# A fused attention, MLP and gated MLP on one core: where loads, adding transfers and a store stand on their queues

## The chip, the core and the metric

The kernel runs on one core of a Trainium2 chip. Its time is the device time of one execution in microseconds (us). TensorE (PE in the profile) multiplies matrices, VectorE (DVE), ScalarE (ACT) and GpSimd (POOL) work on elements, and SyncE (SP) only issues transfers here. GpSimd issues transfers too. Each engine works through its own instructions in order, and so does the queue of issues on SyncE and on GpSimd: an issue that waits holds up those behind it on the same engine.

## The reference

Three stages follow each other, all in 32-bit floats. q, k and v are [4 batches, 8 heads, 576 positions, 64]; x then is [4, 576, 512].

```
s1 = 1/8 * mean4(q) @ mean4(k).T            # means over 4 neighbouring positions, 144 x 144
up = repeat(softmax(s1) @ mean4(v), 4)
s2 = where(|i - j| < 4, 1/8 * q @ k.T, -1e9)
x  = up + softmax(s2) @ v                    # heads side by side: [4, 576, 512]

xn = (x - mean(x)) / sqrt(var(x) + 1e-6) * g
x2 = x + relu(xn @ w_ch1) @ w_ch2            # 512 -> 2048 -> 512

xk = mu_k * x2 + (1 - mu_k) * previous(x2)   # previous position
xr = mu_r * x2 + (1 - mu_r) * previous(x2)
out = sigmoid(xr @ w_r) * (relu(xk @ w_k)**2 @ w_v)   # 512 -> 1024 -> 512
```

## The kernel before

The 2304 positions (4 x 576) are cut into six chunks of 384, `c` = 0 to 5. Activations lie with features on the partitions. Each product of the two MLPs is made of three matmuls with operands split into a high and a low part (`mm3`, L203 to L206).

**Attention** is done in units `(c, hp)`, one for each chunk and each pair of heads (`hp` = 0 to 3), 24 in all. A unit (`unit`, L283) is a generator that gives the engines back at each `yield`. It makes the scores of the mean branch (tile `scd`, L333, from `kd`, the k summed over four positions) and of the local window (`sc`, L337), softmax on VectorE and ScalarE (`P`, `Pd`), transposes (`T`, `PT`, `tp`, `PdT`), and at last the product with v (`av`: L403 with `v`, L412 with `vd`, the v summed over four). Two units are under way at a time. The first chunk's four units run before the MLP starts; those of chunk c + 1 are mixed into the MLP of chunk c by class `Attn` and `slot`.

**Loads of a unit** are issued by SyncE: `load_qk` (L222: tiles `q` and `kz`), `load_v` (L231, tile `v`). `q` and `v` have two buffers each. In `unit` both are called at the start of a unit for the next one, so the load of v for unit u + 1 waits until `av` of unit u - 1 has read its buffer.

**kd and vd** are made for each batch and pair of heads by four transfers each (`sums`, L241): r = 0 is a plain load on SyncE, r = 1 to 3 are adding transfers on GpSimd's queue, each of which waits for the one before it to land. Seven buffers hold them (L237, L238); 16 pairs are made, four of them in the first chunk by sums on VectorE and GpSimd (`first_k`, `first_v`). A unit starts the sums for the unit two places ahead and takes a step of it four times (`step`). New batches begin in chunks 0, 1, 3 and 4.

**Weights** of the first MLP arrive raw (512 KB loads, `raw`, L124 for pairs and L129 for the last ones) and are converted by `conv_gen` in four steps on ScalarE and VectorE: L80, L81, L84, L85, and split into high and low (L88, L91). That goes on during the first chunk's attention and the first chunk of the MLP. Raw pairs and converted weights share 16 buffers (`wpool`). Two pairs are loaded ahead (`AHEAD`); `fetch` then asks for a pair at every second conversion.

**The MLP** of a chunk is `emit_l1` (hidden tile f: `h_ps`, then `hh` on ScalarE L589 and `hl` on VectorE L590) and `emit_l2` (into four accumulators `acc`), for f = 0 to 15. At a chunk's end `emit_x2` (L604) forms x2: VectorE scales `acc` into `x2t` (L609, two buffers), GpSimd adds it to x (L610), and one transfer on SyncE stores all four parts (L611, 768 KB) to `x2d`. The second MLP (from L792) reads `x2d` back, with its own weights that `pre_b` and `load_b` prepare.

A scheduler sets the order of the instructions on each engine from the order in which they are written. An instruction that is passed to `in_order(True, ...)` keeps its written place; others may move past their neighbours on their engine.

Of the kernel before, what the change touches and what calls it, by code (L numbers as in the profile page):

```python
# [23 lines left out]
N = 96 * NG  # L24
NCH = B * S // N
NHP = H // 2
# [3 lines left out]
KT = DM // 128  # L30
# [8 lines left out]
def tile_block(ctx: ExitStack, tc: tile.TileContext, qw, kw, kf, kr, vw, vr, vec, mask, w1, w2, wk, wv, wr, out):  # L39
    nc = tc.nc  # L40
# [15 lines left out]
    x2d = dram.tile([128, KT, B * S], F32, name="x2d")  # L56
# [10 lines left out]
    def in_order(on, ins):  # L67
        if on:
            tc.keep_in_program_order(ins)
# [5 lines left out]
    def decode(raw, pinned=False):  # L75

        top = raw.bitcast(U8).rearrange("p (n t) -> p n t", t=8)[:, :, 3]
        rm = stg.tile([128, 2, 512], U32, tag="stg", name="rm", bufs=RB)
        ru, m = rm[:, 0], rm[:, 1]
        in_order(pinned, nc.scalar.activation(ru.bitcast(F32), raw.rearrange("p (n t) -> p n t", t=2)[:, :, 1].bitcast(F32), AF.Copy, scale=2.0 ** -112))  # L80
        in_order(pinned, nc.vector.tensor_scalar(m, ru, 0x80000000, None, op0=ALU.bitwise_and))  # L81
        yield ru.bitcast(F32)
        low = m.bitcast(U8).rearrange("p (n t) -> p n t", t=4)[:, :, 0]
        in_order(pinned, nc.scalar.activation(low, top, AF.Copy, scale=1.0 / 32.0, bias=-31.0 / 64.0))  # L84
        in_order(pinned, nc.vector.scalar_tensor_tensor(ru, ru, 3, m, op0=ALU.logical_shift_left, op1=ALU.bitwise_or))  # L85

    def split_hi(hi, w):
        return nc.scalar.copy(hi, w)  # L88
# [4 lines left out]
    def wtiles(nm):  # L93
        return [wpool.tile([128, 4, 512], F32R, tag="w", name=f"{nm}{t}") for t in "hl"]
# [7 lines left out]
    def pieces_w12():  # L102
        for p in range(4):
            yield from (("w1", p, k) for k in range(KT))
            yield from (("w2", f // 4, f % 4) for f in range(max(4 * p - 1, 0), 4 * p + 3 if p < 3 else NF))

    def conv_gen():
        keys = list(pieces_w12())
        late_keys = [k for k in keys if k[:2] == ("w2", 3)]
        raws, todo = {}, iter([k for k in keys if k not in late_keys])  # L110

        def fetch():
            key = next(todo, None)
            while key in raws:
                key = next(todo, None)
            if key is None:
                return
            nm, p, k = key
            src = w1s[:, :, 1024 * p:1024 * p + 1024] if nm == "w1" else w2s[:, 4 * p:4 * p + 4, :]
            t = wpool.tile([128, 2, 1024], I32, tag="w", name="raw")  # L120
            for i in range(2):
                raws[nm, p, k + i] = t[:, i]
            for i in range(2):
                in_order(len(raws) < 18, nc.sync.dma_start(t[:, i], src[:, k + i]))  # L124

        def fetch_late(key):
            if key in late_keys:
                t = stg.tile([128, 1024], I32, tag="stg", name="raw", bufs=RB)
                nc.sync.dma_start(t, w2s[:, 12 + key[2], :])  # L129
                raws[key] = t  # L130

        for _ in range(ORDER.count("w")):
            fetch()
            yield
        for _ in range(AHEAD - ORDER.count("w")):
            fetch()
        last = None
        for n, key in enumerate(keys + [None]):
            pin = n < PINNED
            if last:  # L140
                in_order(pin, split_hi(h, w))
            if key:
                nm, p, k = key
                W = W1 if nm == "w1" else W2
                if p not in W:
                    W[p] = wtiles(f"{nm}_{p}")
                g = decode(raws[key], pin)
                w1st = next(g)
            yield
            if key:  # L150
                next(g, None)
            if last:
                in_order(pin, split_lo(h, l, w))
                done.add(last)
            if key:
                h, l, w = W[p][0][:, k, :], W[p][1][:, k, :], w1st
            last = key
            if n % 2 == 1 or n > 24:
                fetch()
            if n + 1 < len(keys):  # L160
                fetch_late(keys[n + 1])
            yield
# [45 lines left out]


    loaded, kds, vdt, vts = {}, {}, {}, {}  # L210
    qds, adding, firsts, raw_k, means = {}, {}, [], {}, {}
    xt, xsum, stage = {}, {}, {}
    av_user, multiplied = [], set()
    PT = pone.tile([128, 2 * NG, 4, 24], F32, name="PT")
# [4 lines left out]
    def runs(c):  # L219
        return [(2 * c + i) // 3 for i in range(2)]  # L220
# [10 lines left out]
    def load_v(c, hp):  # L231
        v = pin.tile([128, NG, 2, D], F32, tag="v", name="v")
        in_order(c == 0, nc.sync.dma_start(v, vw[hp, :, NG * c:NG * c + NG]))
        vts[c, hp] = v
# [6 lines left out]
    def sums(c, hp):  # L241

        new = [(b, *sum_tiles(b, hp)) for b in dict.fromkeys(runs(c)) if (b, hp) not in kds]
        for r in range(4):
            for b, kd, vd in new:
                eng, op = (nc.gpsimd, {"accum_op": ALU.add}) if r else (nc.sync, {})
                in_order(c <= 1 and r > 0, eng.dma_start(kd, kr[b, hp, r], **op))  # L247
                in_order(c <= 1 and r > 0, eng.dma_start(vd, vr[b, hp, r], **op))  # L248
            yield

    def first_k(hp):

# [7 lines left out]
    def first_v(hp):  # L260
        t = xp.tile([128, KT, N], F32, tag=("ah", "al")[hp % 2], name="vr", bufs=1).rearrange("p k n -> p (k n)")[0:KD, 0:1024].rearrange("p (r t d) -> p r t d", r=4, t=2)
        in_order(True, nc.sync.dma_start(t, vr[0, hp].rearrange("r p t d -> p r t d")))
        nc.gpsimd.tensor_tensor(t[:, 0:2], t[:, 0:2], t[:, 2:4], op=ALU.add)
        nc.gpsimd.tensor_tensor(vdt[0, hp], t[:, 0], t[:, 1], op=ALU.add)
# [13 lines left out]
    def mean_of(c, hp):  # L278
        if hp == 0:
            means[c] = ps_h.tile([128, 512], F32, tag="h", name="mean")  # L280
        nc.tensor.matmul(means[c][:, 0:N], ones_r.bitcast(F32), xt[c][:, hp, :], start=hp == 0, stop=hp == NHP - 1)

    def unit(c, hp, nxt):  # L283
        if (c, hp) not in qds:
            prep(c, hp)
        if nxt is not None:
            if nxt not in loaded:
                load_qk(*nxt)
                if nxt[0] == 0:
                    first_k(nxt[1])  # L290
            if nxt not in vts:
                load_v(*nxt)
                if nxt[0] == 0:
                    first_v(nxt[1])
        i = units.index((c, hp)) + 2
        far = units[i] if i < len(units) else None
        if far is not None and far not in adding:
            adding[far] = sums(*far)
        step = lambda: next(adding[far], None) if far is not None else None
        step()  # L300
        new = c == 0 or runs(c)[1] != runs(c - 1)[1]
        q, k = loaded.pop((c, hp))
        v = vts.pop((c, hp))
        if hp == 0:
            xt[c] = xp.tile([128, NHP, N], F32, tag="x", name="x")
        x = xt[c]
        i = hp % 2
        P = Ps[i]
        qd = qds.pop((c, hp))
        kd = [kds[b, hp] for b in runs(c)]  # L310
        vd = [vdt[b, hp] for b in runs(c)]
# [22 lines left out]
        for n in range(NG):  # L334
            for j in range(4):
                o = 24 * j
# [14 lines left out]
            prep(*nxt)  # L351
        yield 900
        stage[c, hp] = 1
        step()
        nc.vector.tensor_reduce(mx[:, 0:2 * NG], Pl, axis=AX.X, op=ALU.max)
        yield 320
        nc.vector.tensor_tensor(Pl, Pl, mx[:, 0:2 * NG].unsqueeze(2).to_broadcast([128, 2 * NG, WIN]), op=ALU.subtract)
# [6 lines left out]
        for j in range(2):  # L364
            nc.scalar.activation(Pd[:, j, :], Pd[:, j, :], AF.Copy, scale=m[:, j:j + 1])
        yield 400
        step()
        nc.vector.tensor_reduce(sm[:, 0:2 * NG], P[:, :, 0:WIN + 1], axis=AX.X, op=ALU.add)
        nc.vector.reciprocal(mx[:, 0:2 * NG], sm[:, 0:2 * NG])
        yield 500  # L370
# [1 line left out]
        yield 340  # L372
        while c + hp > 0 and units[units.index((c, hp)) - 1] not in multiplied:
            yield GAP
        step()
        T = pat.tile([128, 2 * NG, 32], F32, tag="T", name="T", bufs=1)
        nc.vector.transpose(T, P)  # L377
        yield 370
# [18 lines left out]
        yield GAP  # L397
        if c == 0 and hp > 0:
            mean_of(c, hp - 1)
        av = ps_at.tile([128, 512], F32, tag="av", name="av")  # L400
        for n in range(NG):
            for h in range(2):
# [36 lines left out]
    units = [(c, hp) for c in range(NCH) for hp in range(NHP)]  # L439
# [164 lines left out]
    def emit_x2(c):  # L604
        x = xt.pop(c)
        y = rstd.pop(c)
        for o in range(KT):
            t = xp.tile([128, N], F32, tag="x2", name="x2t")
            nc.vector.tensor_tensor(t, acc[o][:, 0:N], y, op=ALU.mult)  # L609
            nc.gpsimd.tensor_tensor(x[:, o, :], t, x[:, o, :], op=ALU.add)  # L610
        nc.sync.dma_start(x2d[:, :, N * c:N * c + N], x)  # L611

    class Feeder:
        def __init__(self, steps):
# [24 lines left out]
    for i in range(2):  # L639
        eng = nc.gpsimd if i else nc.vector  # L640
# [11 lines left out]
    for o in ORDER:  # L652
# [8 lines left out]
            nc.sync.dma_start(vec_t, vec)  # L661
        else:
            next(conv)
    adding.update((u, iter(())) for u in units[0:NHP])
    first = Attn(None, 0)
    i = 0
    while not first.over():
# [124 lines left out]
    for c in range(NCB):  # L792
        for f in range(NK):
            ps = bank()
            wh, wl = WK[f // 4]
            o = 128 * (f % 4)
            for k in range(KT):
                mm3(ps[:, 0:NB], wh[:, k, o:o + 128], wl[:, k, o:o + 128], xk[0][:, k, :], xk[1][:, k, :], k == 0, k == KT - 1)
            r = bp.tile([128, NB], F32, tag="kr", name="kr", bufs=3)
# [4 lines left out]
            kr = r  # L804
# [3 lines left out]
        nxt = Feeder(mix(c + 1, 0)) if c + 1 < NCB else Feeder(iter(()))  # L808
# [101 lines left out]
```

## Time and profile before

| what | value |
|---|---|
| median of 3 runs | 795.38 us (795.38 to 796.32) |
| the profiled execution | 795.89 us |
| its span, first to last instruction | 794.1 us |
| TensorE busy | 752.4 us |
| VectorE, ScalarE, GpSimd busy | 513.0, 370.7, 99.3 us |
| mean granted clock of TensorE | 0.987 of 2.4 GHz |
| moved by transfers | 78.79 MB |

Busy times of different engines overlap. A span of one engine's idle time tells what it waited for last; the chain of waits follows the work that ended last back to the start. The granted clock has two levels, 1.2 and 2.4 GHz; a mean of 0.9 over a stretch says that a fifth of it ran at the lower one.

### The profile page before, as it was taken

How to read it: one execution, taken by the hardware profiler on the slowest of the kernel's cores; microseconds unless marked ns; L12 is line 12 of the kernel's file. 1: busy time of each engine (PE TensorE's matmuls, PEld its weight loads, DVE VectorE, ACT ScalarE, POOL GpSimd, SP SyncE). 2: the span in 40 equal slices, each digit the busy share in tenths (PEclk: the TensorE clock that was granted, in tenths of full speed). 3: DMA queues.
4: the chain of work that ended last, by engine and by line, in shares of the span. 5: the costliest groups of instructions: out<-in, count | busy, mean ns of one | idle time of the engine just before them, and what ended most of it. 6: DMA issues, size and time to landing. Idle time of an engine off the chain costs nothing.

```text
span 794.1 us, 13626 instructions
## 1 busy us (share of the span) xinstructions
PE 752.4 (95%) x5380; PEld 722.6 (91%) x5380; DVE 513.0 (65%) x1015; ACT 370.7 (47%) x839; POOL 99.3 (13%) x124
## 2 busy tenths in 40 slices
PE   3669979899999999999999999999999999999998
PEld 2449869799999999999999999999999999999998
DVE  6777688766546655655555446625969596868664
ACT  4577587645434453445345324524444353525140
POOL 2334123413340001110100010001000000000000
PEclk9969999999999999999999999999999999999999
DMA  8894786446633421553134003403020202010101
GB/s 242 248 249 85 217 232 167 118 139 169 161 71 129 128 96 67 145 138 100 67 101 142 1 1 133 133 1 120 6 75 11 70 1 80 1 40 1 41 1 40
DMA packets 49023, 78.79 MB, mean 99 GB/s; under 512 B 5568, under 2 KB 34880, under 8 KB 48960
## 3 DMA queue, kind: packets, MB, share of 16 engines
q1 hardware_dynamic: 40320, 72.61, 29.0%
q0 software_dynamic: 8640, 5.32, 5.1%
q8 instruction: 42, 0.69, 0.3%
q14 instruction: 21, 0.17, 0.1%
HBM read 63.22 MB, written 14.68 MB: 98 GB/s over the span
## 4 chain that ended last, share of the span: by engine, by line
PE 83%; DMA 5%; ACT 5%; DVE 4%; issue 1%; SPq 1%; POOL 0%; ACTq 0%; POOLq 0%
PE b_ps L206 11%; PE b_ps L204 10%; PE b_ps L205 10%; PE h_ps L204 8%; PE h_ps L205 7%; PE h_ps L206 7%; PE acc L204 7%; PE acc L205 7%; PE acc L206 7%; PE av L403 2%; DMA raw<-in_w 2%; PE scd L333 1%; DMA vd<-in_vr 1%; DMA q<-in_qw 1%; PE sc L337 1%; ACT PT L381 1%
## 5 line engine op out<-in xcount | busy, mean ns | idle before, releaser
L590 DVE SCALAR_TENSOR_TENSOR hl<-h_ps,hh 128x384 fp32r<-128x384 f32 x96 | 53.0, 553 | 94.3 <-ACT hh L589 94.0
L589 ACT ACTIVATE hh<-h_ps 128x384 fp32r<-128x384 f32 x96 | 46.9, 489 | 104.3 <-PE h_ps L206 103.9
L206 PE MATMUL b_ps<-k,wbl 128*128 128x384 f32 x192 | 64.1, 334 | 0.0
L204 PE MATMUL b_ps<-xk,wbh 128*128 128x384 f32 x192 | 64.1, 334 | 0.0
L205 PE MATMUL b_ps<-xk,wbh 128*128 128x384 f32 x192 | 64.1, 334 | 0.0
L206 PE MATMUL b_ps<-xk,wbl 128*128 128x384 f32 x192 | 64.1, 334 | 0.0
L204 PE MATMUL b_ps<-k,wbh 128*128 128x384 f32 x192 | 64.1, 334 | 0.0
L205 PE MATMUL b_ps<-k,wbh 128*128 128x384 f32 x192 | 64.1, 334 | 0.0
L820 DVE RECIPROCAL e<-e 128x384 f32<-128x384 f32 x24 | 61.1, 2544 | 0.1
L610 POOL TENSOR_TENSOR x<-x2t,x 128x384 f32<-128x384 f32 x24 | 23.9, 1058 | 254.4 <-DVE x2t L609 132.2
L737 ACT ACTIVATE mixa<-x2in,vec_t 128x384 f32<-128x384 f32 x48 | 28.1, 612 | 39.7 <-DVE xr L740 33.9
L248 POOL DMA_DIRECT2D vd<-in_vr x36 | 35.1, 991 | 90.9 <-DMA vd<-in_vr 74.1
L381 ACT COPY PT<-T 32x192 f32<-32x192 f32 x96 | 33.4, 348 | 25.5 <-DVE T L377 22.9
L247 POOL DMA_DIRECT2D kd<-in_kr x36 | 35.6, 1013 | 65.8 <-DMA kd<-in_kr 60.0
L800 ACT ACTIVATE kr<-b_ps 128x384 f32<-128x384 f32 x48 | 23.5, 490 | 43.5 <-PE b_ps L206 43.5
L85 DVE SCALAR_TENSOR_TENSOR rm<-rm 128x512 uint32<-128x512 uint32 x52 | 35.7, 688 | 11.2 <-ACT rm L84 10.4
L801 DVE TENSOR_TENSOR kr<-kr,b_ps 128x384 f32<-128x384 f32 x48 | 26.5, 553 | 23.4 <-ACT kr L800 23.4
L84 ACT ACTIVATE rm<-raw 128x512 uint8<-128x512 uint8 x52 | 40.5, 784 | 2.1 <-DVE rm L81 1.9
L790 DVE TENSOR_TENSOR k<-kr,k 128x384 fp32r<-128x384 f32 x48 | 26.7, 557 | 20.3 <-ACT k L789 20.3
L347 ACT ACTIVATE Pd<-scd,mx 96x144 f32<-96x144 f32 x48 | 17.7, 372 | 44.2 <-DVE mx L344 43.7
L80 ACT ACTIVATE rm<-raw 128x512 f32<-128x512 f32 x52 | 34.3, 662 | 6.0 <-DMA raw<-in_w 5.7
L204 PE MATMUL h_ps<-ah,w_2h 128*128 128x384 f32 x96 | 34.6, 360 | 1.9 <-ACT w_2h L88 1.9
(162 smaller groups left out, 2266.6 us busy)
## 6 DMA issues: line engine op xcount, KB each, us to landing
raw<-in_w SPq DMA_DIRECT2D x32, 512.0 KB, 9.5
v<-in_vw SPq DMA_DIRECT2D x24, 256.0 KB, 2.7
bd<-rm SPq DMA_DIRECT2D x20, 256.0 KB, 2.3
wf<-bd SPq DMA_DIRECT2D x10, 512.0 KB, 3.6
q<-in_qw SPq DMA_DIRECT2D x24, 208.0 KB, 2.7
kz<-in_kw SPq DMA_DIRECT2D x48, 102.0 KB, 3.4
x2d<-x SPq DMA_DIRECT2D x6, 768.0 KB
out<-ot SPq DMA_DIRECT2D x24, 192.0 KB, 2.4
```

Source lines behind the costliest of these rows:

```text
L80: in_order(pinned, nc.scalar.activation(ru.bitcast(F32), raw.rearrange("p (n t) -> p n t", t=2)[:, :, 1].bitcast(F32), AF.Copy, scale=2.0 ...
L84: in_order(pinned, nc.scalar.activation(low, top, AF.Copy, scale=1.0 / 32.0, bias=-31.0 / 64.0))
L85: in_order(pinned, nc.vector.scalar_tensor_tensor(ru, ru, 3, m, op0=ALU.logical_shift_left, op1=ALU.bitwise_or))
L204: nc.tensor.matmul(ps, wh, ah, start=first, stop=False)
L205: nc.tensor.matmul(ps, wh, al, start=False, stop=False)
L206: nc.tensor.matmul(ps, wl, ah, start=False, stop=last)
L247: in_order(c <= 1 and r > 0, eng.dma_start(kd, kr[b, hp, r], **op))
L248: in_order(c <= 1 and r > 0, eng.dma_start(vd, vr[b, hp, r], **op))
L381: nc.scalar.copy(PT[p, :, j, :], T[p, :, 0:24])
L589: nc.scalar.activation(hh, ps[:, 0:N], AF.Relu)
L590: last_hl[0] = nc.vector.scalar_tensor_tensor(hl, ps[:, 0:N], 0.0, hh.bitcast(F32), op0=ALU.max, op1=ALU.subtract)
L820: nc.vector.reciprocal(e, e)
```

## The change

Five edits:

1. In `unit`, `load_v` for the next unit (and `first_v` in the first chunk) is called after the loop that waits until the unit before has issued its `av` products, and no longer at the start. The unit takes its own `v` just ahead of its `av` product.
2. The sums for the unit two places ahead are queued in a list, `chains`, at that same place; `tick` takes one step of the first of them, at the same four places as before. Units without new sums have no step.
3. All adding transfers on GpSimd keep their written order, where only those of chunks 0 and 1 did. Raw weight loads keep theirs only for the first four pairs.
4. One more raw pair is fetched at the fifth conversion, so three pairs are ahead from there.
5. x is stored by four transfers of 192 KB on GpSimd's queue.

```diff
-                in_order(len(raws) < 18, nc.sync.dma_start(t[:, i], src[:, k + i]))
+                in_order(len(raws) < 9, nc.sync.dma_start(t[:, i], src[:, k + i]))
...
-            if n % 2 == 1 or n > 24:
+            if n % 2 == 1 or n > 24 or n == 4:
                 fetch()
...
-                in_order(c <= 1 and r > 0, eng.dma_start(kd, kr[b, hp, r], **op))
-                in_order(c <= 1 and r > 0, eng.dma_start(vd, vr[b, hp, r], **op))
-            yield
+                in_order(r > 0, eng.dma_start(kd, kr[b, hp, r], **op))
+                in_order(r > 0, eng.dma_start(vd, vr[b, hp, r], **op))
+            if new:
+                yield True
+
+    def tick():
+        while chains and next(chains[0], None) is None:
+            chains.pop(0)
...
-            if nxt not in vts:
-                load_v(*nxt)
-                if nxt[0] == 0:
-                    first_v(nxt[1])
-        i = units.index((c, hp)) + 2
-        far = units[i] if i < len(units) else None
-        if far is not None and far not in adding:
-            adding[far] = sums(*far)
-        step = lambda: next(adding[far], None) if far is not None else None
-        step()
+        tick()
         new = c == 0 or runs(c)[1] != runs(c - 1)[1]
         q, k = loaded.pop((c, hp))
-        v = vts.pop((c, hp))
...
         while c + hp > 0 and units[units.index((c, hp)) - 1] not in multiplied:
             yield GAP
-        step()
+
+        if nxt is not None and nxt not in vts:
+            load_v(*nxt)
+            if nxt[0] == 0:
+                first_v(nxt[1])
+        i = units.index((c, hp)) + 2
+        if NHP <= i < len(units):
+            chains.append(sums(*units[i]))
+        tick()
         T = pat.tile([128, 2 * NG, 32], F32, tag="T", name="T", bufs=1)
...
+        v = vts.pop((c, hp))
         av = ps_at.tile([128, 512], F32, tag="av", name="av")
...
-        nc.sync.dma_start(x2d[:, :, N * c:N * c + N], x)
+        for o in range(KT):
+            nc.gpsimd.dma_start(x2d[:, o, N * c:N * c + N], x[:, o, :])
```

The two other calls of `step` become `tick`, and the line that gave the first chunk's units empty sums goes.

**Order on SyncE's queue**, from the end of the first chunk's attention into the first chunk of the MLP. `raw<-in_w` are weight loads, `v<-in_vw` loads of v, `kd` and `vd` the r = 0 loads. Before:

```order
L124 DMA raw<-in_w 128x1024 x2
L228 DMA kz_105<-in_kw 64x408
L233 DMA v<-in_vw 128x512
L247 DMA kd<-in_kr 128x144
L248 DMA vd<-in_vr 72x256
L124 DMA raw<-in_w 128x1024 x4
L247 DMA kd<-in_kr 128x144
L224 DMA q<-in_qw 128x416
L228 DMA kz_104<-in_kw 64x408 x2
L233 DMA v<-in_vw 128x512
L248 DMA vd<-in_vr 72x256
L124 DMA raw<-in_w 128x1024 x6
```

With the change:

```order
L124 DMA raw<-in_w 128x1024 x2
L224 DMA q<-in_qw 128x416
L228 DMA kz_105<-in_kw 64x408 x2
L124 DMA raw<-in_w 128x1024 x6
L233 DMA v<-in_vw 128x512
L224 DMA q<-in_qw 128x416
L228 DMA kz_104<-in_kw 64x408 x2
L247 DMA kd<-in_kr 128x144
L248 DMA vd<-in_vr 72x256
L247 DMA kd<-in_kr 128x144
L124 DMA raw<-in_w 128x1024 x6
L233 DMA v<-in_vw 128x512
```

The last load of v in the piece before and the last one in the piece after are the same load, that of unit (1, 2). Counted from the start of the queue, 14 raw loads stood ahead of it, and 24 do now.

**Order on GpSimd** around the first chunk's additions to x (L610, now L614). Before:

```order
L247 DMA kd<-in_kr 128x144
L248 DMA vd<-in_vr 72x256
L247 DMA kd<-in_kr 128x144 x2
L248 DMA vd<-in_vr 72x256 x3
L610 TENSOR_TENSOR x<-x2t,x 128x384 x4
L247 DMA kd<-in_kr 128x144 x3
L248 DMA vd<-in_vr 72x256 x2
```

With the change:

```order
L247 DMA kd<-in_kr 128x144
L248 DMA vd<-in_vr 72x256
L614 TENSOR_TENSOR x<-x2t,x 128x384
L616 DMA x2d<-x 128x384
L614 TENSOR_TENSOR x<-x2t,x 128x384 x2
L616 DMA x2d<-x 128x384
L614 TENSOR_TENSOR x<-x2t,x 128x384
L616 DMA x2d<-x 128x384 x2
L247 DMA kd<-in_kr 128x144
```

From the start of the queue 42 adding transfers stood ahead of these additions, and 24 do now; the first store stands between the first and the second addition.

**Order on VectorE** in the first chunk's attention, from unit 2's masked local scores (`P_108`) on. `qdz_107` and `kd<-kf` are unit 3's sums of q and of k, `scd` the scores that need them. Before:

```order
L345 TENSOR_TENSOR P_108<-sc,mask_t 128x8x30
L355 TENSOR_REDUCE mx<-P_108 128x8
L362 TENSOR_SCALAR sm<-sm 96x2
L357 TENSOR_TENSOR P_108<-P_108,mx 128x8x30
L272 TENSOR_REDUCE qdz_107<-q 64x2x48 x2
L363 RECIPROCAL mx<-sm 96x2
L368 TENSOR_REDUCE sm<-P_108 128x8
L369 RECIPROCAL mx<-sm 128x8
L81 TENSOR_SCALAR rm<-rm 128x512
L371 TENSOR_TENSOR P_108<-P_108,mx 128x8x30
L377 STREAM_TRANSPOSE T<-P_108 128x256
L275 TENSOR_REDUCE kd<-kf 128x144
```

With the change:

```order
L340 TENSOR_TENSOR P_108<-sc,mask_t 128x8x30
L277 TENSOR_REDUCE qdz_107<-q 64x2x48 x2
L280 TENSOR_REDUCE kd<-kf 128x144
L350 TENSOR_REDUCE mx<-P_108 128x8
L357 TENSOR_SCALAR sm<-sm 96x2
L352 TENSOR_TENSOR P_108<-P_108,mx 128x8x30
L358 RECIPROCAL mx<-sm 96x2
L338 TENSOR_REDUCE mx<-scd 96x2
L363 TENSOR_REDUCE sm<-P_108 128x8
L339 TENSOR_SCALAR mx<-mx 96x2
L340 TENSOR_TENSOR P_109<-sc,mask_t 128x8x30
L364 RECIPROCAL mx<-sm 128x8
```

Unit 3's two sums stood behind unit 2's softmax and transpose, and stand ahead of it now; unit 3's own softmax is mixed into unit 2's.

## Rows read from the trace of the kernel before

**Rows 1.** Page, part 1: busy time, share of the span and instructions by engine

```profile
PE 752.4 (95%) x5380; PEld 722.6 (91%) x5380; DVE 513.0 (65%) x1015; ACT 370.7 (47%) x839; POOL 99.3 (13%) x124
```

**Rows 2.** Busy time by stretch: stretch, us, engines, granted clock, DMA share, GB/s

```profile
0.00:60.00 60.00, 31.87 (x279) 22.65 (x280) 41.82 (x98) 34.91 (x84) 19.41 (x33) 0.87 0.89 246
60.00:90.00 30.00, 30.00 (x247) 28.04 (x246) 21.23 (x47) 18.52 (x41) 10.46 (x12) 0.98 0.44 94
90.00:160.00 70.00, 61.28 (x457) 55.04 (x456) 56.66 (x121) 51.56 (x109) 23.04 (x26) 0.98 0.69 190
160.00:780.00 620.00, 618.62 (x4343) 606.55 (x4342) 389.50 (x747) 265.72 (x605) 46.37 (x54) 1.00 0.25 76
```

**Rows 3.** The same view, columns PE, PEld, DVE, ACT, POOL, 20 us each

```profile
90.00:110.00 20.00, 17.13 (x115) 14.54 (x114) 16.36 (x35) 18.56 (x39) 3.80 (x5) 1.00 0.89 278
110.00:130.00 20.00, 17.74 (x146) 16.46 (x145) 17.10 (x39) 14.91 (x33) 8.25 (x10) 0.91 0.76 186
140.00:160.00 20.00, 16.41 (x112) 14.71 (x111) 14.62 (x27) 11.20 (x22) 7.44 (x9) 1.00 0.42 113
```

**Rows 4.** Chain that ended last, 75 to 165 us: start, us, what

```profile
86.53 7.11 DMA raw<-in_w
...
110.77 5.55 DMA raw<-in_w
...
154.57 0.84 POOL vd L248
```

**Rows 5.** Waits of SyncE's queue, 60 to 150 us: total, times, longest

```profile
SPq L233 <- PE av L412: 33.8, 4, 13.4
SPq L247 <- PE scd L333: 20.3, 3, 15.2
```

**Rows 6.** Timeline of SyncE's issues: start, us, what

```profile
84.16 0.33 SPq L233 DMA_DIRECT2D v<-in_vw  x1
...
110.34 0.34 SPq L247 DMA_DIRECT2D kd<-in_kr  x1
```

**Rows 7.** Busy time by stretch, 84 to 94 us

```profile
84.00:94.00 10.00, 10.00 (x103) 9.68 (x100) 7.06 (x17) 4.41 (x12) 1.79 (x2) 1.00 0.85 258
```

**Rows 8.** Timeline of TensorE, 145 to 165 us; in brackets idle before, and releaser

```profile
150.59 0.44 PE L205 MATMUL h_ps<-al,w_0h 128*128 128x384 f32 x1 [1.49 <-DVE al L482]
...
158.53 0.44 PE L205 MATMUL acc<-hl,w_0h 128*128 128x384 f32 x1 [1.57 <-DVE hl L590]
```

**Rows 9.** Timeline of VectorE, 0 to 62 us

```profile
32.42 1.10 DVE L272 TENSOR_REDUCE qdz<-q 64x96 f32<-64x384 f32 x2
...
36.04 0.71 DVE L275 TENSOR_REDUCE kd<-kf 128x144 f32<-128x576 f32 x1
...
46.00 0.68 DVE L91 TENSOR_TENSOR w_0l<-rm,w_0h 128x512 fp32r<-128x512 f32 x1
```

**Rows 10.** Page and transfers: a GpSimd issue (busy, mean ns); two transfers (us to landing)

```profile
L247 POOL DMA_DIRECT2D kd<-in_kr x36 | 35.6, 1013 | 65.8 <-DMA kd<-in_kr 60.0
...
v<-in_vw SPq DMA_DIRECT2D x24, 256.0 KB, 2.7
...
kd<-in_kr POOLq DMA_DIRECT2D x36, 72.0 KB, 4.0
```

**Rows 11.** Timeline of VectorE at the second chunk's end

```profile
237.03 0.56 DVE L590 SCALAR_TENSOR_TENSOR hl<-h_ps,hh 128x384 fp32r<-128x384 f32 x1 [0.33 <-ACT hh L589]
```

**Rows 12.** Timeline of TensorE at the second chunk's end

```profile
238.57 0.33 PE L205 MATMUL acc<-hl,w_0h 128*128 128x384 f32 x1
```

**Rows 13.** Chain that ended last, 240 to 262 us: scores of units (3, 0) and (3, 1)

```profile
243.75 0.49 PE scd L333 x4
...
258.51 0.49 PE scd L333 x4
```

**Rows 14.** Timeline of GpSimd at the second chunk's end

```profile
234.12 3.93 POOL L610 TENSOR_TENSOR x<-x2t,x 128x384 f32<-128x384 f32 x4 [4.28 <-DVE x2t L609]
```

**Rows 15.** Waits, whole span: GpSimd's adding transfers of vd

```profile
POOL vd L248 <- DMA vd<-in_vr: 74.1, 24, 8.7
```

More of the change, by code (lines that the diff above doesn't have):

```diff
@@ L210, in tile_block @@
     loaded, kds, vdt, vts = {}, {}, {}, {}
-    qds, adding, firsts, raw_k, means = {}, {}, [], {}, {}
+    qds, chains, firsts, raw_k, means = {}, [], [], {}, {}
     xt, xsum, stage = {}, {}, {}
@@ L366, in unit @@
         yield 400
-        step()
+        tick()
         nc.vector.tensor_reduce(sm[:, 0:2 * NG], P[:, :, 0:WIN + 1], axis=AX.X, op=ALU.add)
@@ L374, in unit @@
             yield GAP
-        step()
+        if nxt is not None and nxt not in vts:
[5 more added lines that the diff above has]
+            chains.append(sums(*units[i]))
+        tick()
         T = pat.tile([128, 2 * NG, 32], F32, tag="T", name="T", bufs=1)
@@ L663, in tile_block @@
             next(conv)
-    adding.update((u, iter(())) for u in units[0:NHP])
     first = Attn(None, 0)
```

## The prediction

> **What bounds the kernel now.** I read the page's head first, then busy time by stretch, then the chain and the waits of the stretch that loses time. TensorE is busy for 95% of the span of 794.1 us, the other engines for 65% at most [rows 1]. So only TensorE's gaps can be won. By stretch [rows 2] they lie in two places. In the first 60 us (the attention units of the first chunk) TensorE stands idle for 28.1 us; from 90 to 160 us (the rest of the first chunk of the MLP, with weights still being converted) for 70 - 61.28 = 8.7 us. From 60 to 90 us it has none, and from 160 to 780 us 1.4 us in all. The last 14 us hold the final store. A change of the queues can therefore win in the first 160 us, and lose anywhere.
>
> The middle stretch in pieces [rows 3]: 2.87 us idle from 90 to 110 us, 2.26 from 110 to 130, 3.59 from 140 to 160. From 110 to 130 us the mean granted clock is 0.91, so some 18% of 20 us, 3.6 us, ran at the lower level of 1.2 GHz in place of 2.4, which costs about half of it: 1.8 us. It fell after TensorE had stood idle. Together 2.87 + 2.26 + 3.59 + 1.8 = 10.5 us.
>
> What is late there is told by the chain [rows 4]: a raw weight load ends it at 86.5 us (7.11 us) and at 110.8 us (5.55 us); at 154.6 us it is GpSimd's last adding transfer, and behind it the additions to x and VectorE's hl. Why are the loads late? SyncE's queue is in order. From 60 to 150 us it stood 33.8 us in front of loads of v whose buffer an attention product still held, 13.4 us the longest, and 20.3 us in front of kd loads that waited for a scores product [rows 5]. The issues show it [rows 6]: a load of v goes out at 84.16 us, and six raw loads right behind it; a kd load goes out at 110.34 us, again with raw loads next. ScalarE is busy for 4.41 us of the ten from 84 to 94 us: it has nothing to convert [rows 7].
>
> **The change part by part.**
>
> *Loads of v and of r = 0 behind the product, raw loads kept on SyncE's queue.* By the order above, 24 raw loads now stand ahead of the load of v that held up the queue (counted from the start), where 14 did. No transfer is added, so the raw loads come earlier by up to the wait in front of them. What ends first is A = 2.87 + 2.26 idle + 1.8 of clock = 6.9 us. What is late next is the conversion itself: from 90 to 160 us VectorE is busy 56.66 of 70 us and ScalarE 51.56 [rows 2]; with 7 us less these would be 90% and 82%. That is room, but thin, since conversion, attention and the hidden layer take turns on both. I take three quarters, 5.2 us (bounds: half and all of it, 3.4 to 6.9).
>
> *Weights three pairs ahead* is one more fetch at the fifth conversion; it adds no load and works in the same place, so it is in A.
>
> *Adding transfers.* 42 of them stood ahead of the first chunk's additions to x on GpSimd's queue; now 24 do. The wait that they caused ends on TensorE as 1.57 us in front of hl at 158.5 us [rows 8]: B = 1.6 us, all of it (bounds 0.8 to 1.6). The rest of 140 to 160 us, 3.59 - 1.57 = 2.0 us, is mostly the split of the next chunk's x behind the last conversions (1.49 us at 150.6 us [rows 8]). Conversions that end sooner free half of it, I say: C = 1.0 us (0 to 2.0).
>
> *The price at the front.* In the first chunk the q-sums and the k-sum of unit 3 move ahead of unit 2's softmax on VectorE. They take 1.10 and 0.71 us [rows 9], so unit 2 is 1.8 us later; and where the loads land late, a conversion's two steps (L91 takes 0.68 us, L85 as much) come in between as well, 3.2 us in all. Against that, unit 3's scores can start sooner, by 36.04 - 32.42 = 3.6 us at most, since its k-sum still follows the q-sums. The bounds are 3.2 us lost and 3.6 won. I take 1.0 us lost, since VectorE is the busier of the two there (41.8 us of 60 [rows 2]) and a chain that shares it gains little from a head start: D = -1.0.
>
> *The store of x by GpSimd.* One 768 KB issue on SyncE becomes four on GpSimd, 24 in all. An issue takes 1.01 us there [rows 10], so some 24 us on an engine that is 13% busy [rows 1]. What waits: the additions. The second addition now starts behind the first store's issue, and VectorE's fourth x2t needs it, with hl behind that. At the end of the second chunk hl ends at 237.03 + 0.56 = 237.59 us and TensorE takes it at 238.57 [rows 11, 12]: 0.98 us of cover, and 0.33 us more in which hl waited for ScalarE anyway. An issue of 1.01 us fits, so 0; bounds 0 and 0.25 at each of five ends, 1.2 us. x2d is read only by the second layer, after the last chunk's attention.
>
> A sentence of the Trainium skill speaks against this part. Its page DMA: Bandwidth & Descriptors, section Issuing engines are not separate DMA queues, says that transfers from all queues run on the same 16 engines and that starting them from several engines saves only the time to start them. By it nothing would come of the queues' order, and the sum would be B less the price at the front, 0.6 us. The trace does not agree: what [rows 5] show is not the time to start a transfer but the time in which an issue waits and holds those behind it, 13.4 us against 1.
>
> *v later.* A load of v lands in 2.7 us [rows 10], and its product comes a unit after the one that frees the buffer (two units' scores stand 14.8 us apart, [rows 13]): 0.
>
> *Sum.* The profiled execution took 795.9 us (its span is 794.1). 5.2 + 1.6 + 1.0 - 1.0 = 6.8, so 789.1; the median of the runs is 0.5 us below the profiled one, so **788.6 us**. With every bound on one side: 795.4 - 6.9 - 1.6 - 2.0 - 3.6 = 781.3, and 795.4 - 3.4 - 0.8 + 3.2 + 1.2 = 795.6, neither likely.
>
> **The rivals.**
>
> *The converters take over.* If VectorE and ScalarE cannot work faster than they do from 90 to 130 us (33.46 and 33.47 us of 40 [rows 3]), A gives a quarter, 1.7 us, and C nothing: 795.4 - 1.7 - 1.6 + 1.0 = 793.1 us. For it speaks ScalarE's 18.56 of 20 us from 90 to 110 us; against it, that this was catching up after ten idle microseconds. Chance 0.14.
>
> *The raw loads are bound by the DMA engines.* If the queues' order hardly matters, because the transfers themselves take their time, A and C are nothing and B and D remain: 795.4 - 1.6 + 1.0 = 794.8 us. For it speaks a DMA share of 0.89 in the first 60 us [rows 2]; against it, 0.44 from 60 to 90 us, just while the queue stood still. The skill's rule above gives this case. Chance 0.08.
>
> *Adding transfers late: slower.* In chunks of new batches (c = 3 and 4) three adding rounds for a unit now stand on GpSimd behind the chunk's additions and stores. At the second chunk's end GpSimd begins at 234.12 us [rows 14], and the unit's scores come at 258.51 [rows 13]: 24.4 us, less 3.93 for the additions and 4 x 1.01 for the issues leaves 16.4. A round lands in 4.0 us [rows 10], three take 12: a cover of 4.4 us. If, behind 768 KB of stores on its own queue, each round took the longest wait seen, 8.7 us [rows 15], the scores would be 26.1 - 16.4 = 9.7 us late at two places: 795.4 - 6.8 + 19.4 = 808 us. It turns the sign above (16.4 + 3.4) / 3 = 6.6 us a round. The 24 waits of that row have a mean of 3.1 us. Chance 0.09.
>
> **How the numbers follow.** My forecast has 0.69. About 0.2% (1.6 us) is what a measurement can tell from no change, so faster means below 793.8 us. The forecast gives 0.67 to faster and 0.02 to the same; the converters 0.11 and 0.03; the bound loads 0.06 to the same and 0.02 to slower; the late adding transfers 0.09 to slower. Faster 0.78, same 0.11, slower 0.11. The range, 782.5 to 794.5 us, leaves out the late transfers, half of the bound loads and some 0.07 of my own case's ends.
>
> **What would show it.** Right: no wait of SyncE for an attention product above some 3 us before 120 us; raw loads no longer in the chain from 85 to 135 us; ScalarE without a gap of 5 us there; TensorE's idle time from 90 to 160 us near 3 us, its clock at 1.00 throughout, and the additions to x of the first chunk right behind x2t. The first 60 us keep their 28 us of idle TensorE, within 3. Wrong: scores that wait for kd from GpSimd at the third unit or later, hl late at every chunk's end, or raw loads that are issued early and land late.

## The result and the profile after

The change takes 788.55 us (median of 4 runs, 786.69 to 790.81) where the kernel before takes 795.38 (795.05 to 796.32, 4 runs): ratio 0.9913, 95% interval 0.9886 to 0.9941. That is 6.8 us faster; the prediction had 788.6 us. The profiled execution is the slowest of the four: 790.81 us, span 789.0.

Busy time by stretch, with the change (columns as in [rows 2, 3]; the last row answers to [rows 7]):

```profile
0.00:60.00 60.00, 27.12 (x265) 18.51 (x265) 40.88 (x92) 32.50 (x80) 18.61 (x32) 1.00 0.90 255
60.00:90.00 30.00, 30.00 (x202) 27.62 (x203) 26.52 (x58) 26.54 (x54) 6.86 (x8) 1.00 0.68 198
90.00:160.00 70.00, 68.12 (x578) 64.45 (x577) 58.17 (x129) 49.72 (x113) 16.38 (x20) 1.00 0.49 139
160.00:780.00 620.00, 617.61 (x4309) 606.00 (x4309) 388.61 (x736) 263.12 (x596) 71.20 (x89) 1.00 0.27 76
...
90.00:110.00 20.00, 18.66 (x164) 17.23 (x166) 18.48 (x41) 18.54 (x42) 7.50 (x9) 1.00 0.80 200
110.00:130.00 20.00, 19.47 (x195) 18.45 (x195) 18.67 (x46) 15.70 (x39) 0.00 (x0) 1.00 0.43 138
140.00:160.00 20.00, 19.99 (x143) 19.13 (x142) 14.12 (x30) 8.16 (x19) 8.88 (x11) 1.00 0.27 76
...
84.00:94.00 10.00, 9.32 (x108) 8.38 (x108) 9.70 (x20) 9.39 (x19) 2.80 (x4) 1.00 0.98 295
```

From 90 to 160 us TensorE is idle for 1.88 us instead of 8.72; ScalarE is busy for 9.39 us of the ten in which it had 4.41. The first 60 us got worse: 32.9 us idle instead of 28.1. SyncE's queue, its waits from 60 to 150 us (total, times, longest) and its issues:

```profile
SPq L224 <- PE sc L332: 21.6, 3, 18.1
SPq L233 <- PE av L416: 17.9, 3, 8.7
```

```profile
73.96 0.33 SPq L224 DMA_DIRECT2D q<-in_qw  x1
...
77.89 3.70 SPq L124 DMA_DIRECT2D raw<-in_w  x6
89.36 0.33 SPq L233 DMA_DIRECT2D v<-in_vw  x1
```

The queue still stands still, 18.1 us in front of a load of q (before, 13.4 in front of v [rows 5]). But six raw loads now go out ahead of the load of v, at 77.89 us. In the kernel before they came behind it:

```profile
84.97 3.73 SPq L124 DMA_DIRECT2D raw<-in_w  x6
```

GpSimd at the first chunk's end:

```profile
148.53 1.02 POOL L614 TENSOR_TENSOR x<-x2t,x 128x384 f32<-128x384 f32 x1 [40.57 <-DVE x2t L613]
149.95 0.61 POOL L616 DMA_DIRECT2D x2d<-x  x1 [0.41 <-POOL x L614]
```

The additions stand right behind x2t (before, adding transfers kept GpSimd until 155 us [rows 4]), and a store's issue takes 0.6 us, not the 1.01 of an adding transfer.

### The profile page after: what moved, and what is told of

Same layout as the page of the kernel before. It is cut to its first block, busy times and chain, and to the rows that moved or that the text cites. A ratio compares the mean times of both kernels' runs of the same rounds, so it can differ in the third digit from the quotient of the medians.

```text
span 789.0 us, 13649 instructions
## 1 busy us (share of the span) xinstructions
PE 748.5 (95%) x5380; PEld 721.9 (91%) x5380; DVE 515.3 (65%) x1015; ACT 371.9 (47%) x839; POOL 113.1 (14%) x148
## 4 chain that ended last, share of the span: by engine, by line
PE 83%; DVE 6%; ACT 5%; DMA 3%; SPq 1%; issue 1%; ACTq 0%
PE b_ps L206 11%; PE b_ps L204 11%; PE b_ps L205 11%; PE h_ps L204 8%; PE h_ps L205 7%; PE h_ps L206 7%; PE acc L204 7%; PE acc L205 7%; PE acc L206 7%; PE av L407 2%; DMA q<-in_qw 2%; ACT PT L384 1%; PE sc L332 1%; ACT rm L84 1%; PE scd L328 1%; DMA raw<-in_w 1%
## 5 line engine op out<-in xcount | busy, mean ns | idle before, releaser
L614 POOL TENSOR_TENSOR x<-x2t,x 128x384 f32<-128x384 f32 x24 | 24.3, 1028 | 301.5 <-DVE x2t L613 301.3
L248 POOL DMA_DIRECT2D vd<-in_vr x36 | 38.8, 1079 | 14.2 <-DMA vd<-in_vr 13.8
L407 PEld LDWEIGHTS av<-PT,v 128*64 128x64 f32 x384 | 18.9, 151 | 20.0 <-ACT PT L384 13.9
```

The lines of the kernel that those rows point to most:

```text
L248: in_order(r > 0, eng.dma_start(vd, vr[b, hp, r], **op))
L407: in_order(n + h, nc.tensor.matmul(av[64 * h:64 * h + 64, 96 * n:96 * n + 96], v[:, n, h, :], PT[:, NG * h + n, :, :], start=True, stop=Tr ...
```

## The experiments

Two questions. What lets the raw loads pass: the moved loads of v, as predicted, or one of the other edits? And what does the front pay? "Ahead" is the number of raw loads written on SyncE's queue ahead of the load of v that stood at 84 us; "at" is when the block of raw loads behind the q and kz loads near 70 us goes out.

| run | us, median (range) | ratio, 95% interval | ahead | at, us |
|---|---|---|---|---|
| before | 795.4 to 797.6 | | 14 | 84.97 |
| the change | 788.55 (786.69 to 790.81) | 0.9913 (0.9886 to 0.9941) | 24 | 77.89 |
| e1 extra pair | 788.04 (786.38 to 789.32) | 0.9894 (0.9870 to 0.9917) | 24 | 72.28 |
| e2 v moved | 799.92 (797.69 to 803.12) | 1.0049 (1.0031 to 1.0067) | 14 | 87.77 |
| e3 adds moved | 796.20 (792.98 to 798.84) | 0.9998 (0.9980 to 1.0015) | 14 | 86.26 |
| e4 v at old place | 786.75 (786.49 to 788.09) | 0.9878 (0.9850 to 0.9906) | 24 | 75.27 |
| e5 three buffers | 796.98 (795.40 to 798.93) | 0.9991 (0.9977 to 1.0005) | 14 | 84.82 |
| e6 raws unpinned | 789.49 (788.03 to 794.08) | 0.9897 (0.9871 to 0.9923) | 21 | 71.42 |
| e7 first chunk's v old | 787.20 (786.82 to 787.57) | 0.9863 (0.9845 to 0.9881) | 24 | 74.39 |
| e8 load early, sums late | 789.90 (789.11 to 790.58) | 0.9896 (0.9878 to 0.9915) | 24 | 75.92 |
| e9 no raw edits | 786.76 (785.87 to 787.21) | 0.9871 (0.9844 to 0.9897) | 22 | 69.17 |
| e10 extra pair, store | 789.33 (787.38 to 792.68) | 0.9917 (0.9887 to 0.9948) | 24 | 72.41 |
| e11 sums early, load late | 785.94 (785.10 to 786.93) | 0.9863 (0.9836 to 0.9890) | 24 | 74.53 |
| e12 one v sum left out | 786.89 (786.37 to 787.38) | 0.9881 (0.9863 to 0.9899) | 24 | 73.13 |

Runs e1 to e4, e5 to e8 and e9 to e11 each shared a chip and its runs of the kernel before; the change and e12 have such runs of their own.

### What lets the raw loads pass

**e1, the extra pair alone**, on the kernel before:

```diff
-            if n % 2 == 1 or n > 24:
+            if n % 2 == 1 or n > 24 or n == 4:
```

> The kernel before with one edit of the change alone: the raw pair fetched at the fifth conversion. In the written order of SyncE's queue 24 raw loads then stand ahead of the load of v for the seventh unit listed, as with the whole change, where 14 did. Theory 1 (the prediction's step: the moved loads of v free the queue, the extra pair adds nothing of its own): 795.4 us within 0.8, TensorE's idle time from 90 to 160 us stays near 8.7 us. Theory 2 (the extra pair alone brings the raw loads forward): A without the adding transfers and without the price at the front, 795.4 - 5.2 = 790 us, idle time from 90 to 160 us 3 to 5 us, SyncE still waits for av, but with nothing urgent behind.

It gains all that the change gains. SyncE's issues:

```profile
72.28 4.03 SPq L124 DMA_DIRECT2D raw<-in_w  x6
85.55 0.33 SPq L233 DMA_DIRECT2D v<-in_vw  x1
```

The load of v still goes out at 85.55 us, as late as before, and SyncE still stands up to 9.3 us in front of a load of v; the raw loads are past it.

**e2, the loads of v moved alone**, on the kernel before (the call moves from the unit's start to behind the wait for the products):

```diff
-            if nxt not in vts:
-                load_v(*nxt)
...
             yield GAP
-        step()
+        if nxt is not None and nxt not in vts:
+            load_v(*nxt)
```

> The kernel before with the loads of v (and the first chunk's sums for v) moved behind the products, and nothing else. In the written order 14 raw loads still stand ahead of that load of v. Theory 1 (moved loads of v win A): 795.4 - 5.2 + 1.0 for the front = 791.2 us, idle time from 90 to 160 us 3 to 5 us. Theory 2 (the extra pair wins A): no gain, 795 to 798 us, idle time from 90 to 160 us near 8.7 us and 1 to 3 us more of it in the first 60 us, where unit 2 comes later.

No gain; at 0.5% slower it is slower than either theory had it. The raw loads stay behind the load of v:

```profile
86.95 0.33 SPq L233 DMA_DIRECT2D v<-in_vw  x1
87.39 0.34 SPq L248 DMA_DIRECT2D vd<-in_vr  x1
87.77 4.38 SPq L124 DMA_DIRECT2D raw<-in_w  x6
```

**e3, the adding transfers' list and kept order alone** (`chains`, `tick`, `in_order(r > 0, ...)`; everything else as before):

> The kernel before with the adding transfers' list and their kept order alone; loads of v, raw loads and the store of x as before. Both theories of the raw loads: B alone, 795.4 - 1.6 = 793.8 us, the first chunk's additions to x right behind x2t, TensorE's wait for hl near 158 us gone. The rival of late adding transfers: slower than 796.5 us, scores of the third unit of chunks 3 and 4 wait for kd.

A miss for both. TensorE's wait for hl behind 145 us [rows 8] is gone from its trace, one for al remains (1.30 us at 152.15), and the additions begin at 154.84 us, right behind x2t. The time is that of the kernel before. From the first x2t to the end this trace takes 641.1 us, the kernel before 641.5: of the wait of 1.57 us only 0.4 shows there. The hidden layer also reaches full pace later, at 63.3 us instead of 61.2; why wasn't tried.

**e5, three buffers for v**, on the kernel before:

```diff
-        v = pin.tile([128, NG, 2, D], F32, tag="v", name="v")
+        v = pin.tile([128, NG, 2, D], F32, tag="v", name="v", bufs=3)
```

> The kernel before with three buffers for v in place of two, and nothing else: a load of v then waits for the product of the unit before the last, not the last, so that SyncE's waits for av go, while the raw pairs are asked for as before (two ahead). If those waits are what holds the raw loads (the step of the prediction, taken alone): SyncE's wait for av from 60 to 150 us falls from 33.8 us to below 10, TensorE's idle time from 90 to 160 us from 8.7 to 3 to 5 us, 790 us. If what is wanted is that raw loads are asked for earlier (the extra pair): the waits go or pass to the kd loads behind them (20.3 us before), and the time stays within 1.5 us of the kernel before.

The edit did not take the wait away. The scheduler put the next unit's load of v in the same place, and SyncE waited there as before:

```profile
84.00 0.34 SPq L233 DMA_DIRECT2D v<-in_vw  x1
84.44 0.34 SPq L248 DMA_DIRECT2D vd<-in_vr  x1
84.82 4.22 SPq L124 DMA_DIRECT2D raw<-in_w  x6
```

So it says nothing on a queue without that wait; with order and wait unchanged, the time is too.

**e6, the raw loads unpinned alone**, on the kernel before:

```diff
-                in_order(len(raws) < 18, nc.sync.dma_start(t[:, i], src[:, k + i]))
+                in_order(len(raws) < 9, nc.sync.dma_start(t[:, i], src[:, k + i]))
```

> The kernel before, but only the first four raw pairs keep their written order on SyncE's queue (nine pairs before); no extra pair, loads of v as before. 21 raw loads then stand ahead of the load of v that had 14. If the place on the queue decides: most of A, 790 to 792 us, idle time from 90 to 160 us 3 to 6 us. If the extra pair's lead decides (its buffer is asked for earlier): no change, 795 to 797.5 us.

All of A again, with no extra pair: it is the place on the queue, not the lead.

**e9, the change without both edits on raw loads**:

```diff
-                in_order(len(raws) < 9, nc.sync.dma_start(t[:, i], src[:, k + i]))
+                in_order(len(raws) < 18, nc.sync.dma_start(t[:, i], src[:, k + i]))
...
-            if n % 2 == 1 or n > 24 or n == 4:
+            if n % 2 == 1 or n > 24:
```

> The whole change without its two edits on raw loads: nine raw pairs keep their written order, and no extra pair is fetched. What is left is the loads of v and the r = 0 loads behind the products, the kept order of the adding transfers and the store by GpSimd. 22 raw loads stand ahead of the load of v that had 14 before, as 24 do in the change, although each of the two moves by itself leaves 14. If that place on the queue is all that matters: A stays, 0.990 to 0.993 of the kernel before. If the extra pair or the freed order of the raw loads has to be there: 0.998 to 1.005.

A is all there, though e2 and e3, its two halves, gained nothing (the store by GpSimd, which e9 has besides, begins only behind 144 us). Moved together, the loads of v and the r = 0 loads go behind a whole block:

```profile
69.17 5.31 SPq L124 DMA_DIRECT2D raw<-in_w  x8
89.37 0.33 SPq L224 DMA_DIRECT2D q<-in_qw  x1
...
90.91 0.58 SPq L233 DMA_DIRECT2D v<-in_vw  x1
```

The table splits cleanly: with 14 ahead the block goes out at 84.8 us or later and the ratio is 0.999 or more; with 21 or more, at 77.9 us or sooner, and it is 0.992 or less. Three ways lead there, each enough: the extra pair, the freed order, or both moves together.

### What the front pays

**e4, the change with all loads of v and the first chunk's sums at the old place**, and **e7, with those of the first chunk only**:

```diff
                 load_qk(*nxt)
                 if nxt[0] == 0:
                     first_k(nxt[1])
+            if nxt not in vts and nxt[0] == 0:
+                load_v(*nxt)
+                if nxt[0] == 0:
+                    first_v(nxt[1])
```

(e4 without `and nxt[0] == 0`, and without the later call.)

> The whole change, but the loads of v and the first chunk's sums for v called at the start of a unit, as before. Theory 1: A is lost again, 788.6 + 5.2 - 1.0 = 792.8 us, SyncE waits 10 us and more for av between 60 and 120 us and raw loads come late. Theory 2: A stays and the price at the front goes, 788.6 - 1 to 2 = 787 us; idle time of the first 60 us back near 28 us, that from 90 to 160 us near 2 us.

> The whole change, but the first chunk's loads of v and sums for v are called at the start of a unit as before; those of the later chunks behind the products. If moving the loads of v costs only in the first chunk: as the run with all loads of v at the old place, 0.988 of the kernel before, product of the third unit at 39 to 40.5 us instead of 43.95. If moving the later loads of v wins something of its own: 1 us or more below that. If it costs something: above 0.990.

In time both are as foreseen for a price that sits in the first chunk (theory 2 of e4). The idle time of the first 60 us is not: 31.1 and 31.4 us, where e4 had 28. Where the later chunks' loads of v stand makes no difference that shows.

**e8, the load of v early and the sums late**, and **e11, the sums early and the load late** (of the lines above only `load_v`, or only `first_v`):

> The whole change, but the first chunk's loads of v alone are called at the start of a unit; the transfer of vr and GpSimd's sums for v stay behind the products. If the price at the front comes from the late sums on GpSimd, which stretch VectorE's steps while they run (1.43 and 1.51 us for steps of 0.40 us in the third unit): little comes back, 0.990 to 0.992 of the kernel before, third unit's product at 43 us or later. If it comes from the loads of v standing late on SyncE's queue, ahead of others: 0.988 and 40 us.

> The counterpart of the run with the loads of v early: the whole change, but in the first chunk the transfer of vr and GpSimd's sums for v are called at the start of a unit, and the loads of v stay behind the products. If the late sums are what the front pays for: third unit's product at 41 us or sooner, 0.987 to 0.988 of the kernel before. If the late loads of v are: 43 us or later and 0.990 to 0.991.

With the sums early and the loads late (e11) the ratio is that of e7, so the late loads of v cost nothing that shows. That leaves the late sums, but the times alone don't show that they cost anything: e9 has them and is 0.8 us behind e11 on the same chip, with ranges that overlap. The third unit's product comes at 41.30 us in e11 and at 43.95 in the change, but 1.5 of these 2.65 us were there at the first unit's product already (17.35, 18.89). e8 is 2.7 us behind e7 on the same chip, but by a slip in its edit it fetches and sums the second unit's part of v twice (five pairs of additions on GpSimd in its first 60 us, four elsewhere), so it prices nothing. How late sums can cost time in the change, where the third unit's are done by 37.6 us, is what e12 tests.

**e12, the change without the first addition for v**:

```diff
-        nc.gpsimd.tensor_tensor(t[:, 0:2], t[:, 0:2], t[:, 2:4], op=ALU.add)
```

> The whole change without the first of GpSimd's two additions for v in the first chunk's four units (1.27 us each; of the four positions only two are then summed for v there); order on VectorE and SyncE as in the change. If VectorE's long steps in the third unit (1.43, 1.51 and 0.92 us where 0.41 is usual) are stretched by GpSimd's addition running at the same time: none of these steps runs beside a first addition any more, at most one is long by 0.8 us beside the second one, third unit's product 1 to 3 us sooner after its scores than the 8.7 us (35.24 to 43.95) of the change, and 1 to 2.5 us less time, 0.988 to 0.990 of the kernel before. If they are long for another reason: the same long steps and 0.991.

GpSimd and VectorE in the third unit, with the change:

```profile
35.39 1.30 POOL L268 TENSOR_TENSOR vr<-vr 72x512 f32<-72x512 f32 x1 [12.01 <-DMA vr<-in_vr]
36.77 0.78 POOL L269 TENSOR_TENSOR vd<-vr 72x256 f32<-72x256 f32 x1
38.53 1.26 POOL L268 TENSOR_TENSOR vr<-vr 72x512 f32<-72x512 f32 x1 [0.98 <-DMA vr<-in_vr]
```

```profile
35.53 1.43 DVE L352 TENSOR_TENSOR P<-P,mx 128x240 f32<-128x240 f32 x1
...
38.57 1.51 DVE L81 TENSOR_SCALAR rm<-rm 128x512 uint32<-128x512 uint32 x1
40.00 0.92 DVE L366 TENSOR_TENSOR P<-P,mx 128x240 f32<-128x240 f32 x1
```

The same three of VectorE in e12:

```profile
33.30 0.40 DVE L351 TENSOR_TENSOR P<-P,mx 128x240 f32<-128x240 f32 x1
...
35.87 0.42 DVE L81 TENSOR_SCALAR rm<-rm 128x512 uint32<-128x512 uint32 x1
36.20 0.40 DVE L365 TENSOR_TENSOR P<-P,mx 128x240 f32<-128x240 f32 x1
```

With the order unchanged, 3.86 us become 1.22 in sum, and the product comes 6.8 us behind the scores (32.80, 39.63) instead of 8.7. So these steps were long because of GpSimd. The time points the same way; its interval overlaps that of the change.

What the additions meet is not fixed. In e9 they stand at the same place in the code, and VectorE's order in this unit is that of the change, but two small steps meet them. GpSimd and VectorE there:

```profile
34.71 1.27 POOL L268 TENSOR_TENSOR vr<-vr 72x512 f32<-72x512 f32 x1 [12.80 <-DMA vr<-in_vr]
37.50 1.34 POOL L268 TENSOR_TENSOR vr<-vr 72x512 f32<-72x512 f32 x1 [0.71 <-DMA vr<-in_vr]
```

```profile
34.95 1.05 DVE L339 TENSOR_SCALAR mx<-mx 96x2 f32<-96x2 f32 x1
37.65 0.43 DVE L380 STREAM_TRANSPOSE T<-P 128x256 f32<-128x256 f32 x1
38.01 0.86 DVE L357 TENSOR_SCALAR sm<-sm 96x2 f32<-96x2 f32 x1
```

In the change L339 and L357 take 0.17 and 0.12 us where no addition runs, so e9 pays 1.6 us on them and not 2.6 on three. Its product comes 7.0 us behind the scores (33.45, 40.44), and its hidden layer is at full pace at 59.6 us, sooner than in the kernel before (61.2).

### The store

**e10, the extra pair and the store of x by GpSimd** (edits 4 and 5 on the kernel before):

> The kernel before with two edits: the extra raw pair, and x stored by four transfers on GpSimd's queue. The prediction costs the store at nothing, with up to 1.2 us lost: 788 to 789.2 us, as the extra pair alone or slower. From the traces: with the store on GpSimd the second MLP's first product starts 2.3 us before the last chunk's first x2t, against 1.3 us without: 0.9 us won, 787 us, 0.988 of the kernel before.

Inconclusive: 0.9917 against 0.9894 without the store, and the intervals overlap. In the profiled executions the second MLP's first product starts 304.0 us behind the second chunk's last x2t, against 305.5 in e1 and 304.7 in the kernel before, a gain of at most 1.5 us that the times don't show. VectorE's fourth x2t does wait longer for the second addition at that chunk's end (1.54 us, 0.42 in e1), but no loss of an issue's length from chunk to chunk is seen.

## Why the prediction was right, and where its steps were not

**The sum.** Predicted 6.8 us, measured 6.8 by the medians. To the tenth that is luck: the four runs spread over 4.1 us, and the terms missed in both directions. The profiled executions differ by 5.1 us of span. By landmarks: the hidden layer's matmuls reach full pace 5.4 us later (66.6 instead of 61.2), the first x2t comes 4.7 us sooner (147.9 instead of 152.6, so 10.1 won in the middle), and from there to the end it takes 0.4 us less: -5.4 + 10.1 + 0.4 = 5.1.

**A**, 5.2 predicted, is 5.1: idle time from 90 to 130 us falls from 5.13 to 1.87 and the 1.8 us of clock go (granted clock 1.00; of the hidden layer's matmuls from 110 to 130 us none starts 0.30 to 0.34 us ahead of the next, where seven did). **B and C**, 1.6 + 1.0, are 3.6 as gaps: from 140 to 160 us TensorE has none left. Their worth in time is another matter. C's share, 2.0, lies ahead of the first x2t, and A and C make 7.1 of the 10.1. Idle time counts only part of a pause there, since a matmul's record is 0.33 us long and the next one can start 0.17 behind it: what goes beyond 0.174 us from one start to the next, summed over the hidden layer's matmuls between full pace and the first x2t, falls from 13.6 to 4.7 us, 8.9 of the 10.1. B's 1.57 lies behind the first x2t (158.5 against 152.6), where only 0.4 us was won, as in e3: the wait went, and most of its worth did not come.

**The step that failed** is the reason given for A. "No transfer is added, so the raw loads come earlier by up to the wait in front of them" was put on the loads of v and of r = 0 moved behind the product, and of the extra pair it was said that it "adds no load and works in the same place". The moves do win A, but only together (e9); the loads of v alone lose 3 us (e2). The extra pair alone wins all of it (e1), so does freeing the raw loads' order (e6). The change does the same thing three times over, and the prediction credited one of them. What it took from the written order, 24 against 14, was the right measure; it had not been counted for each edit by itself. One reading was off as well: 86.5 and 110.8 us, told as the ends of raw loads, are their starts in [rows 4]. The signs given were half right: the waits for av did not fall below 3 us (8.7 the longest, and 18.1 for q), yet the raw loads left the chain's long pieces and ScalarE its gap. A wait on the queue cost nothing that shows once nothing urgent stood behind it (e1).

**D**, -1.0 (bounds -3.2 to 3.6), was too small in most runs: e2 by itself lost 3.2 us (799.92 - 796.70); within the change it is 2.8 us against e4 (0.9913, 0.9878, intervals that overlap) and 4.0 against e7 (0.9863, whose interval ends just below that of the change); the profiled execution, the slowest of the four, lost 5.4. Some 1.7 us of that is another matter: the first unit's product comes at 18.89 us instead of 17.23 with the order unchanged, behind a conversion that waited 1.85 us for its raw load. "Within 3" of 28 us idle failed with 32.9. The mechanism was half missed: the reorder on VectorE was seen, the late sums on GpSimd and what they do to VectorE were not. The price is not constant: e9 has the same late sums and 0.9871, and in its trace the front ends 1.7 us sooner than in the kernel before. Its additions met smaller steps; whether that is all of the difference is open, and so is the size of D.

**B** by itself (e3) takes the wait for hl away and hardly any time, as told. **The store** at 0 stands. **The rivals**: the converters did not take over (VectorE 18.67 of 20 us from 110 to 130 us, and TensorE idle for 0.5). The raw loads were not bound by the DMA engines: e6 adds and removes no transfer, changes the order alone, and gains 1.0%. So what the prediction drew from the Trainium skill (DMA: Bandwidth & Descriptors, section Issuing engines are not separate DMA queues), that the order of the queues would bring nothing, does not hold here. The sentence itself speaks of transfers started from several engines, not of an issue that waits and holds up those behind it. Late adding transfers did not come: the adding rounds at the second chunk's end are 3.3 us apart (235.46, 238.74, 242.06), below the 6.6 at which that rival turns the sign, and from 160 to 780 us TensorE waits for no kd.

The best version that ran is e11: 785.94 us, ratio 0.9863 (0.9836 to 0.9890). It beats the kernel before; its interval still touches that of the change, and e9 on the same chip is not told apart from it.

## What to carry to other kernels

A wait at the head of an in-order queue has a price only through what stands behind it: count the urgent issues ahead of the waiting one, before and after, and count them for each edit by itself and for the edits together, since edits that each do nothing can do it jointly, and one line can do it alone. Try each edit alone before crediting the one that the story is about. A step moved to GpSimd's idle time need not be free when VectorE is on the path beside it.

## What was not expected of the hardware

**VectorE is held up while GpSimd adds.** Some of VectorE's steps that meet one of GpSimd's additions end just behind it: L352 runs from 35.53 to 36.96 us, where GpSimd's addition ends at 36.69; a usual 0.41 us becomes 1.43. The Trainium skill, SBUF — State Buffer, section Who interferes with whom, says that only the pair of ports that the two share makes them contend, and that it is an exclusive lock. The trace agrees: 2.6 us more on three steps, gone in e12. Not every step is held: in e9 the transpose L380 takes its usual 0.43 us in the middle of an addition.

**The granted clock in the records can miss the slow pace.** TensorE in both kernels while the hidden layer starts, two matmuls at the slow pace and two at the full one. Before:

```profile
59.02 0.52 PE L204 MATMUL h_ps<-ah,w_0h 128*128 128x384 f32 x1
59.34 0.52 PE L205 MATMUL h_ps<-al,w_0h 128*128 128x384 f32 x1
...
61.25 0.34 PE L204 MATMUL h_ps<-ah,w_0h 128*128 128x384 f32 x1
61.42 0.34 PE L205 MATMUL h_ps<-al,w_0h 128*128 128x384 f32 x1
```

With the change:

```profile
63.48 0.52 PE L205 MATMUL h_ps<-al,w_0h 128*128 128x384 f32 x1
63.80 0.52 PE L206 MATMUL h_ps<-ah,w_0l 128*128 128x384 f32 x1
...
66.62 0.34 PE L205 MATMUL h_ps<-al,w_0h 128*128 128x384 f32 x1
66.80 0.34 PE L206 MATMUL h_ps<-ah,w_0l 128*128 128x384 f32 x1
```

They start 0.32 us apart and then 0.17 or 0.18, in both. TensorE's busy time and granted clock in two of these microseconds, before and then with the change:

```profile
58.00:60.00 2.00, 2.00 (x8) 0.50 0.97 369
```

```profile
62.00:64.00 2.00, 2.00 (x8) 1.00 1.03 353
```

Eight matmuls in 2 us both times, and a granted clock of 0.50 in one and 1.00 in the other. So the 1.00 for the first 60 us of the change is no gain; the pace of the matmuls tells. Whether the record missed a spell at the lower level or something else halved the pace, no run here shows.
